# A spectral mixing layer and a SwiGLU block on one core: the back-transform's bursts in 512 columns, its clean-up at other places, and one load a step earlier

## The chip, the core and the metric

The kernel runs on one core of a Trainium2 chip. The metric is the device time of one execution in microseconds. Before the change it is 2777.25 us, the median of three runs (2773.95 to 2780.49). Engines are named as in the profile: PE is TensorE (PEld its weight loads, PEq its sequencer), DVE VectorE, ACT ScalarE, POOL GpSimd, SP SyncE, whose queue (SPq) issues most DMAs. All arithmetic is in float32, and each product that the program states is two matmul instructions in the trace.

## The reference

Two layers, one after the other. x has 8 batches of 3008 tokens with 256 channels.

```python
X = np.fft.rfft(x, axis=1)
y = np.fft.irfft(X * (filt_r + 1j * filt_i), n=3008, axis=1)   # along the tokens
t = y.reshape(24064, 256)
g = t @ w_gate                                                  # 256 -> 1536
out = (g * sigmoid(g) * (t @ w_val)) @ w_out                    # 1536 -> 256
```

## The kernel before

**Work.** A batch goes through two stages that overlap: while the feed-forward part of batch b runs, the spectral part of batch b + 1 is computed in small pieces between its products. The Fourier transform along 3008 = 47 x 64 tokens is split: the first stages (`quads`, `fours`, lines 715 to 881) go there, multiply by the filter and come back as far as a DRAM buffer of 48 x 64 rows (`d2`), and `back` (lines 1029 to 1066) does the last step for a quarter of a batch (a chunk). A batch has four chunks, and a chunk has three groups of hidden columns, so a batch is 12 steps, numbered 0 to 11. Each step is the same list of products: `P`, `Q` and the combinations `A`, `B`, `E` (L1134) make gate and value columns, and the `W` products (L1232) project hidden columns to the output. The products are a fast scheme in which sums of blocks replace some of the products, so DVE, ACT and POOL form sums between them.

**Order.** The order of every step is written by hand: `SCHEDULE` (lines 88 to 96) is a list of tokens, and the loop at line 1511 issues for each token its piece of work. Each engine executes what it gets in that order, and waits for other engines where data or space ask for it. A token with a prime belongs to the step before: its work is left over from there. Tokens that matter here: `h`, `v` are DVE products of hidden values (L1181); `x` and `s` make inputs of `A` on DVE (L1156); `l` (L312) and `e` (L316 or an ACT copy) do so for the `E` products; `S` are sums of hidden tiles on POOL (L309, L312); `n` are sums for the next chunk; `b0` to `b7` advance the spectral piece that this step carries (`quads` in steps 0 to 3, `fours` in steps 4 to 10, the first sums of a batch's x, `first_fold`, in step 11). Batches 0 to 5 have that last piece, and batch 7 has no next batch and carries none of these. In batch 0 the spectral work is arranged differently.

**`back`.** It is a generator of six pieces, called by the tokens `r0`, `r1` in the steps 0, 3 and 6 (for the chunks 1 to 3 of the same batch) and 10 (chunk 0 of the next batch), and by `r2'` to `r5'` in the step after. `r0`: a burst of small products (L1039): 24 rows by 32 columns of a constant table, in four row groups and four column groups of the array, into four PSUM banks. `r1`: DVE transposes two of the banks into the tile `y` (L1046), ACT copies the other two to `odd` (L1051). `r2'`: DVE transposes the two `odd` tiles (L1054). `r3'`, `r4'`: POOL adds and subtracts `odd` and `y` (L1059, L1061; in the profile under the helpers' lines L309 and L312). `r5'`: four more POOL sums on `y`. The tile `y` is first read by `n2` of the step 3k + 2 that precedes its chunk (step 11 for chunk 0). In batch 0 one call, for chunk 0 of batch 1, runs inside the `b` tokens of step 11. There are 28 calls: 21 in the batches 1 to 7, six in step 10 of the batches 1 to 6, and that one.

**Loads.** `load_t4` (lines 661 to 677) brings a chunk's rows of `d2` in two halves of four row blocks each, into two tiles of a pool with two buffers, one half per tile (`t4`). For chunks 1 to 3 the first half is issued at the start of the steps 0, 2 and 5, the second at `B01` of the same step; for chunk 0 of the next batch at `B01` and `A12` of step 10. Each half is four DMAs of 96 KB on SP's queue. `load_x(0)` (lines 615 to 625) loads a piece of x for a later batch: one DMA of 512 KB from a reordered copy (`turned`) and four of 128 KB from x, into a region of the tile `lent` that the filter of `fours` uses in steps up to 9. It is issued at `Q0`, the first token of step 11, and `first_fold` reads it on DVE at `b4` of the same step. SP's queue also carries the reloads of the weights (`wt_t`, L474, four pieces a step) and the stores of the results (L1217, twelve in a row in steps 1, 4, 7 and 10, after their DVE transposes at `z1.o'` and later).

Of the kernel before, what the change touches and what calls it, by code (L numbers as in the profile page):

```python
# [41 lines left out]
FP32 = mybir.dt.float32  # L42
# [6 lines left out]
B, S, C = 8, 3008, 256  # L49
# [5 lines left out]
NS, NQ = 24, 64  # L55
# [3 lines left out]
NH = 4  # L59
NW = 2 * NH  # L60
NCHUNK = 32 // NW
# [3 lines left out]
NG = 3  # L65
# [20 lines left out]


SCHEDULE = """
Q0 o3' z1.o' t4.2' W2 b0 f0 S00' S01' i0 b1 b2 x0.o' r2' t0.0 x1.o' i1 Q1 P0 t0.1 x2.o' P3 x3.o' f1 t4.3'
W1 x4.o' S10' x03 S11' D01 i2 i3 i4 s13 b3 x5.o' P1 o1 b4 t0.2 o2 z0.o c1 i5 A13 g1 c0 S20' Q2  # L90
S21' g0 y01 m13 t1.0 h0 f2 s01 W6 t1.1 h1 x23 D02 P2 o6 D12 A01 t0.3 i6 c2 i7 B13 i8 g2 i9 n3' m01
i10 S30' t1.2 i11 x02 W7 S31' g13 y12 r3' y02 B01 r4' h13 o7 t1.3 t2.0 s02 s12 g01 h2 b5 Q3 t2.1 h01 e12
A02 y23 W4 e02 b6 y03 m02 g3 A12 o4 z2.o t2.2 E12 m12 B02 t2.3 l12 e13 b7 E02 r5' u12 g02 t3.0 h3 s23
l02 B12 v12 E13 t3.1 h02 u02 A23 n2 l13 g12 v02 W5 s03 e23 h12 e01 m23 A03 o5 z3.o u13 E23 t3.2 m03
v13 E01 l23 e03 t3.3 t4.0 l01 u23 B23 v23 u01 E03 n1 t4.1 v01 g23 B03 l03 r0 W3 h23 g03 u03 r1 h03 v03
""".split()
KS = (-1, 0, 1, 2)

# [99 lines left out]
def kernel(  # L198
# [10 lines left out]
    nc = tc.nc  # L209
# [10 lines left out]
    def pool(name, bufs, space=None):  # L220
        kw = {} if space is None else {"space": space}
        return ctx.enter_context(tc.tile_pool(name=name, bufs=bufs, **kw))

    cpool = pool("consts", 1)
    xpool = pool("xp", 2)
    t1pool = pool("t1", 2)
    t4pool = pool("t4", 2)
    ypool = pool("yp", 2)
    wdpool = pool("wdram", 1, DRAM)
    wps = pool("wps", NB, PSUM)  # L230
# [3 lines left out]

    wt_t = cpool.tile([128, NPR, 2, 128], FP32)
    y_t = cpool.tile([128, 3 * len(PAIRS), TQ], FP32)

    lent = cpool.tile([128, 14 * NV * C], FP32)
    wt_1 = lent[:, 0:NPR * 256].rearrange("p (s z f) -> p s z f", z=2, f=128)
# [50 lines left out]
    pin = tc.keep_in_program_order  # L290
# [263 lines left out]
    back_t, quad_t = [], []  # L554
# [23 lines left out]
    class Spectral:  # L578
# [82 lines left out]
        def load_t4(self, k, i, part=None):  # L661
            at = 2 * k + i
            if part:
                self.load_rows(self.t4[k, i][8 * N_STORED:NK], k, slice(2 * N_STORED, NS), ts(i, NH))
                return
            t = t4pool.tile([128, NH, C], FP32, name=f"t4_{self.b}_{k}_{i}", tag="t4")
            if part == 0:
                self.load_rows(t[0:8 * N_STORED], k, slice(0, 2 * N_STORED), ts(i, NH), nc.gpsimd)
            elif self.b == 0:
                self.load_rows(t[0:NK], k, slice(0, NS), ts(i, NH))  # L670
            else:

                rows = self.d2_tokens.rearrange("(h n) (r s) c -> h r s n c", h=2, r=2)
                for part in range(4):
                    self.load(out=t[32 * part:32 * part + NS],
                              in_=rows[part // 2, part % 2, :, ts(at, NH)])
            self.t4[k, i] = t
# [351 lines left out]
        def back(self, k):  # L1029

            self.y[k] = y = ypool.tile([128, 8, TQ], FP32, name=f"y_{self.b}_{k}", tag="y")
            banks = [bank(f"pd_{self.b}_{k}_{part}") for part in range(4)]
            views = [t.rearrange("p (z i n d) -> p i z n d", z=2, i=2, d=32) for t in banks]
            for i in range(2):
                t = self.t4[k, i].rearrange("p n (z j d) -> p j z n d", z=2, d=32)
                for j in range(4):
                    for part in range(4):
                        r = slice(32 * part, 32 * part + NS)
                        pin(nc.tensor.matmul(  # L1039
                            out=views[part][32 * j:32 * j + 32, i], lhsT=back_t[0][r],  # L1040
                            rhs=t[r, j], start=i == 0, stop=True, skip_group_check=True))
            yield
            to = y.rearrange("p s n -> p (s n)").rearrange("p (z h m r) -> p h z m r", z=2, h=2, r=N1)
            odd = []
            for h in range(2):
                pin(nc.vector.transpose(  # L1046
                    out=to[:, h, :, :, 0:32],
                    in_=banks[2 * h].rearrange("p (z m r) -> p z m r", z=2, r=32)))
                t = xpool.tile([128, NV, C], FP32, name=f"odd_{self.b}_{k}_{h}", tag="x")
                odd.append(t.rearrange("p i c -> p (i c)"))  # L1050
                pin(nc.scalar.copy(out=odd[h], in_=banks[2 * h + 1]))  # L1051
            yield
            for t in odd:
                pin(nc.vector.transpose(out=t, in_=t))  # L1054
            yield
            for h in range(2):
                t = odd[h].rearrange("p (z m r) -> p z m r", z=2, r=32)
                n, low = slice(1 - h, 1 - h + N1 - NS), to[:, h, :, :, 0:NS]
                pin(sub(nc.gpsimd, to[:, h, :, :, N1 - 1:NS - 1:-1],  # L1059
                        to[:, h, :, :, n], t[:, :, :, n]))  # L1060
                pin(add(nc.gpsimd, low, low, t[:, :, :, 0:NS]))  # L1061
                yield
            for a in range(4):
                b, v = y[:, a], y[:, 4 + a]
                for _ in range(abs(KS[a])):
                    pin((sub if KS[a] > 0 else add)(nc.gpsimd, v, v, b))
# [191 lines left out]
    x0 = [t[0:NR, 8 * C * i:8 * C * i + 8 * C] for t, i in ((wo_f, 0), (wo_f, 1), (y_f, 0))]  # L1258
# [7 lines left out]
    with tc.tile_pool(name="start", bufs=1) as spool0:  # L1266
# [12 lines left out]
        n = 0  # L1279
# [174 lines left out]
    for b in range(B):  # L1454
# [38 lines left out]
        for step in range(NCHUNK * NG + (b == B - 1)):  # L1493
# [15 lines left out]
            last = ghost or b == B - 1 and step == NCHUNK * NG - 1  # L1509
            place = -1  # L1510
            for token in SCHEDULE:
                place += token[0] != "r"
                if b == 0 and this and place in tick_at[min(step, 3)]:
                    preparation.tick(step)
                old = token.endswith("'")
                op = token.rstrip("'")
                if (b, step) == (0, 0):
                    if op == "A01":
                        idle(wt_t[:, 0:2].rearrange("p s z f -> p (s z f)"),
                             [bank("idle") for _ in range(2)], 512)  # L1520
                    if op == "n2":
                        continue
                    if op == "n1":
                        preparation.finish(1)
                    elif op == "e23":
                        this.step("n2")
                if op[0] == "i":
                    if older is not None and older.b == 0:
                        older.project(op)
                elif op[0] == "t":  # L1530
                    n = int(op[1])
                    ps = pieces_before if old else pieces
                    if n < len(ps):
                        next(ps[n], None)
                elif op[0] == "r":
                    next(back_before if old else backs.get(step, gap), None)
                elif op[0] == "b":
                    next(bursts[step] if this else gap, None)
                elif op[0] in "Wo" or op.endswith(".o"):

                    g0 = older if old else before
                    if g0 is not None and (old or not ghost):
                        g0.project(op)
                else:
                    g0 = before if old else this
                    if g0 is not None and not (ghost and op[0] == "S"):
                        g0.step(op)
                if old or this is None:
                    continue
                if b == 0 and (step, op) == (5, "A23"):  # L1550
                    nxt.load_two(0)
                if b and b + 2 < B and (step, op) == (8, "Q0"):
                    following.turn_rows(0, 1, 2, 3)
                if b + 2 < B and (step, op) == (11, "Q0"):
                    following.load_x(0)
                if b == 1 and step < 4 and op in FILTER_AT:
                    n = FILTER_AT.index(op)
                    keep_filter(4 * step + n)
                if b and chunk and op == "B01":
                    cur.load_t4(chunk, 1)  # L1560
                for i in range(2):
                    if nxt and (step, op) == (10, ("B01", "A12")[i] if b else "E23"):
                        nxt.load_t4(0, i)
                for f, args in chores.get((step, op), ()) if b == 0 else ():
                    f(*args)
                if op in ends and not last and (b or step >= NT * NG - 1):
                    reload_weights((g + 1) % NG, ends[op])
# [35 lines left out]
```

## Time and profile before

| | |
|---|---|
| median of 3 runs | 2777.25 us |
| the profiled execution | 2773.0 us, of which span 2771.2 us |
| PE busy | 2728.7 us, 98% of the span |
| DVE, ACT, POOL busy | 75%, 55%, 63% |
| clock granted to PE over the span | 0.998 |
| `back` products, L1039 | 1792 matmul instructions of 24 x 256 (28 calls of 64), 42.7 us of PE |
| `quads` products, L725 | 768 of 24 x 512 (24 calls of 32), 27.4 us of PE |
| bytes moved by DMA | 608.47 MB, mean 220 GB/s |

Busy time of an engine is the union of its instructions. A row of the timeline is a run of equal instructions: its start, the time from the first start to the last end, line, tiles written and read, their number, and in brackets the idle time before it with what ended it. Matmuls are pipelined, so the distance from one row's start to the next says more than the second column. Idle time of an engine costs only where PE then waits for it.

### The profile page before, as it was taken

What the parts mean: (1) busy time and instruction counts of PE and PEld (TensorE: products, weight loads), DVE (VectorE), ACT (ScalarE), POOL (GpSimd) and SP (SyncE); (2) the same over time, 40 slices, a digit from 0 to 9 for tenths busy, and PEclk for the clock granted to TensorE, in tenths of its full rate; (3) what the DMA queues carried; (4) which work ended last, traced back from release to release, by engine and by line L of the source; (5) the groups of instructions that cost most, each with busy time, mean ns of one, the idle gap of its engine ahead of it and who ended that gap; (6) DMA issues with size and microseconds to landing.
All of it is one profiled execution on the core that took longest, in us unless ns stands there. A gap on an engine that the chain in (4) does not pass through costs nothing.

```text
span 2771.2 us, 51629 instructions
## 1 busy us (share of the span) xinstructions
PE 2728.7 (98%) x16952; PEld 2243.7 (81%) x16952; DVE 2082.3 (75%) x4703; ACT 1535.2 (55%) x4142; POOL 1758.0 (63%) x1909
## 2 busy tenths in 40 slices
PE   8999999999999999999999999999999999999998
PEld 6778887888877888788887888878887888888886
DVE  7788778777687777777778777777777777676666
ACT  5676455555555555555555555555555555555553
POOL 4777576676565766566765676566656566566553
PEclk9999999999999999999999999999999999999999
DMA  8688877877676776777767777668776777654443
GB/s 218 221 265 288 275 244 233 274 243 260 209 205 207 259 247 193 213 229 234 252 193 230 223 243 232 211 192 263 245 222 194 216 244 237 182 159 146 153 145 81
DMA packets 385312, 608.47 MB, mean 220 GB/s; under 512 B 199002, under 2 KB 268536, under 8 KB 384870
## 3 DMA queue, kind: packets, MB, share of 16 engines
q1 hardware_dynamic: 365833, 574.23, 66.0%
q10 hardware_dynamic: 16701, 25.56, 3.7%
q0 software_dynamic: 2512, 5.38, 0.7%
q8 instruction: 137, 2.24, 0.3%
q14 instruction: 129, 1.06, 0.1%
HBM read 484.44 MB, written 118.12 MB: 217 GB/s over the span
## 4 chain that ended last, share of the span: by engine, by line
PE 87%; DVE 4%; ACT 2%; DMA 2%; POOL 1%; issue 1%; SPq 0%; ACTq 0%; POOLq 0%; DVEq 0%
PE wa L1134 24%; PE wk L1134 16%; PE wA L1232 16%; PE we L1134 12%; PE wG L1232 8%; PE wF L1232 4%; PE wpd L1039 1%; PE wqc L805 1%; PE wqb L817 1%; PE wqa L725 1%; DVE we L312 1%; DVE y L316 0%; DVE lent L312 0%; DMA y<-y 0%; DVE h L1181 0%
## 5 line engine op out<-in xcount | busy, mean ns | idle before, releaser
L1134 PE MATMUL wa<-y_t,wt_t 128*128 128x188 f32 x4464 | 882.9, 324 | 15.8 <-DVE wa L1156 8.4
L1134 PEld LDWEIGHTS wa<-y_t,wt_t 128*128 128x128 f32 x4464 | 745.1, 190 | 105.2 <-PE wk L1134 16.6
L1134 PEld LDWEIGHTS wk<-y,wt_t 128*128 128x128 f32 x2976 | 497.3, 190 | 111.2 <-issue 27.5
L1134 PE MATMUL wk<-y,wt_t 128*128 128x188 f32 x2976 | 572.8, 325 | 0.0
L312 POOL TENSOR_TENSOR h<-h 128x376 f32<-128x376 f32 x572 | 561.4, 1003 | 15.1 <-DVE h L309 14.9
L1232 PE MATMUL wA<-h,wo_t 128*128 128x376 f32 x1532 | 548.3, 480 | 0.8 <-DVE o L309 0.7
L309 POOL TENSOR_TENSOR h<-h 128x376 f32<-128x376 f32 x190 | 183.5, 987 | 546.0 <-DVE h L1181 533.6
L1134 PE MATMUL we<-y_t,wt_t 128*128 128x188 f32 x2232 | 432.4, 323 | 2.4 <-DVE we L316 1.6
L312 POOL TENSOR_TENSOR D<-f,f 128x376 f32<-128x376 f32 x288 | 281.8, 990 | 225.2 <-ACT f L1149 219.3
L312 DVE TENSOR_TENSOR we<-we,m 128x376 f32<-128x376 f32 x576 | 317.9, 554 | 111.0 <-PE we L1134 98.1
L1134 PEld LDWEIGHTS we<-y_t,wt_t 128*128 128x128 f32 x2232 | 368.9, 190 | 5.0 <-DVE we L316 2.8
L1232 PEld LDWEIGHTS wA<-h,wo_t 128*128 128x128 f32 x1532 | 277.9, 190 | 102.9 <-POOL h L312 1.8
L1169 ACT COPY m<-wa 128x376 f32<-128x376 f32 x576 | 275.3, 478 | 91.9 <-PE wa L1134 87.4
L1176 ACT ACTIVATE u<-we 128x188 f32<-128x188 f32 x576 | 189.1, 328 | 178.0 <-DVE we L312 171.7
L1232 PE MATMUL wG<-h,wo_t 128*128 128x376 f32 x768 | 276.7, 483 | 0.0
L1176 ACT ACTIVATE g<-wa 128x188 f32<-128x188 f32 x576 | 187.4, 326 | 153.4 <-PE wa L1134 151.0
L316 DVE SCALAR_TENSOR_TENSOR y<-wk,c 128x376 f32<-128x376 f32 x480 | 247.4, 541 | 31.4 <-ACT c L1153 26.5
L1153 ACT COPY c<-wk 128x376 f32<-128x376 f32 x288 | 136.8, 475 | 235.3 <-PE wk L1134 226.7
L1149 ACT ACTIVATE f<-wk 128x376 f32<-128x376 f32 x288 | 144.4, 501 | 159.1 <-PE wk L1134 148.5
L1181 DVE TENSOR_TENSOR h<-we,u 128x188 f32<-128x188 f32 x576 | 199.0, 346 | 38.0 <-ACT u L1176 24.9
L1181 DVE TENSOR_TENSOR h<-wa,g 128x188 f32<-128x188 f32 x576 | 197.8, 344 | 33.8 <-ACT g L1176 33.5
L1165 ACT COPY we<-y 128x376 f32<-128x376 f32 x480 | 216.9, 481 | 5.3 <-DVE h L1181 4.0
(198 smaller groups left out, 3640.8 us busy)
## 6 DMA issues: line engine op xcount, KB each, us to landing
wt_t<-w_all SPq DMA_DIRECT2D x174, 896.0 KB
wt_t<-w_all SPq DMA_DIRECT2D x174, 768.0 KB
lent<-filter SPq DMA_DIRECT2D x36, 1024.0 KB
quads<-lent SPq DMA_DIRECT2D x96, 256.0 KB
d<-lent ACTq DMA_DIRECT2D x84, 256.0 KB
t<-d SPq DMA_DIRECT2D x224, 96.0 KB
lent<-quads SPq DMA_DIRECT2D x144, 128.0 KB
lent<-raw SPq DMA_DIRECT2D x144, 128.0 KB
```

What stands on the lines that cost most here:

```text
L309: return eng.tensor_tensor(out=dst, in0=a, in1=b, op=ALU.add)
L312: return eng.tensor_tensor(out=dst, in0=a, in1=b, op=ALU.subtract)
L316: return nc.vector.scalar_tensor_tensor(out=dst, in0=a, scalar=-1.0, in1=b, op0=ALU.mult, op1=ALU.subtract)
L725: pin(nc.tensor.matmul(out=banks[u, h][c:c + 32], lhsT=quad_t[0][r:r + NS, ts(t, 32)], rhs=parts[t][r:r + NS, ts(cp, NV * C)], start=True, ...
L1134: pin(nc.tensor.matmul(out=ps[:, z], lhsT=self.wt[:, SLOT[p], z], rhs=rhs, start=start and z == 0, stop=True, skip_group_check=True))
L1149: pin(act.mul(self.small(f"f{i}", f"f{i}", 1), t[f"k{i}"], -1.0))
L1153: pin(act.copy(out=self.small(f"c{i}", f"c{i}", 1), in_=t[f"k{i}"]))
L1165: pin(act.copy(out=self.bank(f"e{at}"), in_=t[f"y{at}"]))
L1169: pin(act.copy(out=self.small(f"m{at}", "m", 4), in_=t[f"a{at}"]))
L1176: pin(act.activation(out=self.small(op, "g", 3, 1)[:, 0], in_=ps[:, 1], func=AF.Silu))
L1181: pin(v.tensor_tensor(out=dst, in0=ps[:, 0], in1=g, op=ALU.mult))
L1232: pin(nc.tensor.matmul(out=self.tiles[at], lhsT=wo_t[:, JB * q + i, WO[p], :], rhs=self.hs[i][:, HID[p]], start=start and i == 0, stop=Tru ...
```

## The change

1. The two halves of a chunk's rows go into one constant tile `t4_t` with 2 x 4 row blocks, instead of two tiles from a pool. The places in memory are as large as before.
2. `r0` loops over the four column groups and four row groups only, and each product takes all eight row blocks: 512 columns instead of twice 256. That is 16 products (32 matmul instructions) per call where there were 32 (64). Each product needs both halves of the rows.
3. `r1` stands after `h03 v03`, the last two tokens of a step, instead of ahead of them.
4. `r2'` to `r5'` stand later in the steps 1, 4 and 7: `r2'` between `t2.3` and `l12`, `r3'` after `u12`, `r4'` after `v12`, `r5'` after `A23`. In step 11 they stay where they were, as tokens with a capital `R`, which do nothing in other steps.
5. `load_x(0)` is issued at `Q0` of step 10 instead of step 11 in the batches 1 to 5; in batch 0 it stays in step 11.

```diff
-Q0 o3' z1.o' t4.2' W2 b0 f0 S00' S01' i0 b1 b2 x0.o' r2' t0.0 x1.o' ...
+Q0 o3' z1.o' t4.2' W2 b0 f0 S00' S01' i0 b1 b2 x0.o' R2' t0.0 x1.o' ...
...
-i10 S30' t1.2 i11 x02 W7 S31' g13 y12 r3' y02 B01 r4' h13 o7 t1.3 ...
-A02 y23 W4 e02 b6 y03 m02 g3 A12 o4 z2.o t2.2 E12 m12 B02 t2.3 l12 e13 b7 E02 r5' u12 g02 t3.0 h3 s23
-l02 B12 v12 E13 t3.1 h02 u02 A23 n2 l13 g12 v02 W5 s03 ...
-v13 E01 l23 ... l03 r0 W3 h23 g03 u03 r1 h03 v03
+i10 S30' t1.2 i11 x02 W7 S31' g13 y12 R3' y02 B01 R4' h13 o7 t1.3 ...
+A02 y23 W4 e02 b6 y03 m02 g3 A12 o4 z2.o t2.2 E12 m12 B02 t2.3 r2' l12 e13 b7 E02 R5' u12 r3' g02 t3.0 h3 s23
+l02 B12 v12 r4' E13 t3.1 h02 u02 A23 r5' n2 l13 g12 v02 W5 s03 ...
+v13 E01 l23 ... l03 r0 W3 h23 g03 u03 h03 v03 r1
...
-    t4pool = pool("t4", 2)
...
+    t4_t = cpool.tile([128, 2 * NH, C], FP32)
...
-            t = t4pool.tile([128, NH, C], FP32, name=f"t4_{self.b}_{k}_{i}", tag="t4")
+            t = t4_t[:, ts(i, NH)]
...
-            views = [t.rearrange("p (z i n d) -> p i z n d", z=2, i=2, d=32) for t in banks]
-            for i in range(2):
-                t = self.t4[k, i].rearrange("p n (z j d) -> p j z n d", z=2, d=32)
-                for j in range(4):
-                    for part in range(4):
-                        r = slice(32 * part, 32 * part + NS)
-                        pin(nc.tensor.matmul(
-                            out=views[part][32 * j:32 * j + 32, i], lhsT=back_t[0][r],
-                            rhs=t[r, j], start=i == 0, stop=True, skip_group_check=True))
+            t = t4_t.rearrange("p n (z j d) -> p j z n d", z=2, d=32)
+            for j in range(4):
+                for part in range(4):
+                    r = slice(32 * part, 32 * part + NS)
+                    pin(nc.tensor.matmul(
+                        out=banks[part][32 * j:32 * j + 32].rearrange("p (z n d) -> p z n d", z=2, d=32),
+                        lhsT=back_t[0][r], rhs=t[r, j], start=True, stop=True))
...
-                elif op[0] == "r":
-                    next(back_before if old else backs.get(step, gap), None)
+                elif op[0] in "rR":
+                    if not old:
+                        next(backs.get(step, gap), None)
+                    elif (op[0] == "R") == (step == NCHUNK * NG - 1):
+                        next(back_before, None)
...
-                if b + 2 < B and (step, op) == (11, "Q0"):
+                if b + 2 < B and (step, op) == (10 + (b == 0), "Q0"):
                     following.load_x(0)
```

More of the change, by code (lines that the diff above doesn't have):

```diff
@@ L88 @@
 SCHEDULE = """
-Q0 o3' z1.o' t4.2' W2 b0 f0 S00' S01' i0 b1 b2 x0.o' r2' t0.0 x1.o' i1 Q1 P0 t0.1 x2.o' P3 x3.o' f1 t4.3'
+Q0 o3' z1.o' t4.2' W2 b0 f0 S00' S01' i0 b1 b2 x0.o' R2' t0.0 x1.o' i1 Q1 P0 t0.1 x2.o' P3 x3.o' f1 t4.3'
 W1 x4.o' S10' x03 S11' D01 i2 i3 i4 s13 b3 x5.o' P1 o1 b4 t0.2 o2 z0.o c1 i5 A13 g1 c0 S20' Q2
 S21' g0 y01 m13 t1.0 h0 f2 s01 W6 t1.1 h1 x23 D02 P2 o6 D12 A01 t0.3 i6 c2 i7 B13 i8 g2 i9 n3' m01
-i10 S30' t1.2 i11 x02 W7 S31' g13 y12 r3' y02 B01 r4' h13 o7 t1.3 t2.0 s02 s12 g01 h2 b5 Q3 t2.1 h01 e12
-A02 y23 W4 e02 b6 y03 m02 g3 A12 o4 z2.o t2.2 E12 m12 B02 t2.3 l12 e13 b7 E02 r5' u12 g02 t3.0 h3 s23
-l02 B12 v12 E13 t3.1 h02 u02 A23 n2 l13 g12 v02 W5 s03 e23 h12 e01 m23 A03 o5 z3.o u13 E23 t3.2 m03
-v13 E01 l23 e03 t3.3 t4.0 l01 u23 B23 v23 u01 E03 n1 t4.1 v01 g23 B03 l03 r0 W3 h23 g03 u03 r1 h03 v03
+i10 S30' t1.2 i11 x02 W7 S31' g13 y12 R3' y02 B01 R4' h13 o7 t1.3 t2.0 s02 s12 g01 h2 b5 Q3 t2.1 h01 e12
+A02 y23 W4 e02 b6 y03 m02 g3 A12 o4 z2.o t2.2 E12 m12 B02 t2.3 r2' l12 e13 b7 E02 R5' u12 r3' g02 t3.0 h3 s23
+l02 B12 v12 r4' E13 t3.1 h02 u02 A23 r5' n2 l13 g12 v02 W5 s03 e23 h12 e01 m23 A03 o5 z3.o u13 E23 t3.2 m03
+v13 E01 l23 e03 t3.3 t4.0 l01 u23 B23 v23 u01 E03 n1 t4.1 v01 g23 B03 l03 r0 W3 h23 g03 u03 h03 v03 r1
 """.split()
@@ L1511 @@
             for token in SCHEDULE:
-                place += token[0] != "r"
+                place += token[0] not in "rR"
                 if b == 0 and this and place in tick_at[min(step, 3)]:
```

## The prediction

> **What bounds the kernel.** I read the page first, then TensorE's waits, the chain, and the timelines of PE, DVE and SP around every place that the diff touches. All times are from the profiled execution (2773.0 us, span 2771.2), 4.25 below the median of the runs.
>
> ```profile
> span 2771.2 us, 51629 instructions
> PE 2728.7 (98%) x16952; PEld 2243.7 (81%) x16952; DVE 2082.3 (75%) x4703; ACT 1535.2 (55%) x4142; POOL 1758.0 (63%) x1909
> ```
> PE is the bound: a saving counts if it shortens PE's own work or one of its few waits. The largest wait of PE is
>
> ```profile
> PE wa L1134 <- DVE wa L1156: 8.4, 14, 1.5
> ```
> 14 waits for `s` tokens. The chain shows the price of a `back`: in batch 7, without other spectral work, the same 12 products recur once a step.
>
> ```profile
> 2444.07 1.91 PE wk L1134 x12
> ...
> 2471.08 1.91 PE wk L1134 x12
> ...
> 2496.48 1.91 PE wk L1134 x12
> ```
> A step with `back` takes 27.01 us, the next, which holds `r2'` to `r5'`, 25.40: `back` costs PE 1.61, its later pieces nothing there. The two kinds of burst, before (`back`) and a relative (`quads`), on PE's timeline:
>
> ```profile
> 1747.37 1.49 PE L1039 MATMUL wpd<-t,back 24*32 24x256 f32 x64
> 1748.79 1.53 PE L1232 MATMUL wG<-h,wo_t 128*128 128x376 f32 x4
> ```
>
> ```profile
> 1776.33 1.43 PE L1232 MATMUL wF<-h,wo_t 128*128 128x376 f32 x4
> 1777.68 1.14 PE L725 MATMUL wqa<-lent,quad 24*32 24x512 f32 x32
> 1778.75 2.18 PE L1134 MATMUL wk<-y,wt_t 128*128 128x188 f32 x12
> 1780.77 0.48 PE L1232 MATMUL wA<-h,wo_t 128*128 128x376 f32 x1
> ```
> The reader is to see that the 24x512 burst, exactly the shape of the new one, holds PE for 1.07 from its start to the next row, the old one for 1.42.
>
> **Change 1 and 2: the burst.** Slot of `quads`: 1776.33 to 1780.77 is 4.44; four W matmuls take 1.27 and twelve wk 1.91 elsewhere; 1.26 is left. Slot of `back`: 1.61. Difference 0.35, times 28 calls: **9.8 us**. Why it is so, by single starts in the trace: 16 tiles of the array run together, starting 7 ns apart; a pass of 16 takes 0.216 (second pass, 1747.61 to 1747.82) at 256 columns and 0.453 at 512 (`quads`, first pass). So streaming is the same; gone is the hole between the halves, 1747.82 to 1748.01, where the second half's four loads are waited for, and one filling. The moving operand is strided (runs of 32 floats) where that of `quads` is contiguous; but the old burst's second pass ran 256 strided columns in 0.216, the rate of `quads`, so I cost the stride at nothing.
>
> The Trainium skill's page TensorEngine Tiling (Array Packing), section Key Properties, speaks against the change: a switch of tiling mode drains the array. The trace agrees: the next full-size matmul starts 0.30 after the last start of the old burst, 0.52 after that of `quads`, so longer products make the drain longer by 0.21. Without a drain, the saving would be 0.56 a call and 15.8 in all; the rows above hold it already.
>
> The Trainium skill's TensorE: Matmul & The Clock Gate, section "Wait — 56ns, not 53.3ns?", says starts are never closer than about 25 ns; 32 fewer instructions would be worth 0.8 a call, 22 us in all. The rows' 7 ns contradict it, and I keep 0.35.
>
> What the trace can't show: all eight waits for loads now come ahead of the first products. Before, four stood there as waits of PE's sequencer (0.05 each, issued 0.125 apart, the last one 0.94 before the burst) and four hung on weight loads in the middle. Four more at 0.125 use 0.5 of the 0.94: nothing lost. Bounds of the call's gain: 0.56, were the drain no longer than before; and 0.35 - 4 x 0.125 = -0.15, were the waits not hidden. I take 0.35, whose row has the same shape. Range of the part: -4 to +16.
>
> Loads themselves: the tightest is step 10, where SP issues the eight `t` from 1732.57 to 1737.57 and the burst starts at 1747.37; a similar load of 256 KB on POOL's queue lands in 4.7. That the first products now need both halves costs nothing with 5 us in hand. Each half has the same place in memory as before, so what a new load waits for, the burst several steps back, is long past.
>
> **Change 3: `r1` after `h03 v03`.** The two `h`, `v` (0.34 each) wait for nothing while DVE idles ahead of the burst's end, so they go ahead of the transposes; ACT's order is unchanged. The banks come free no later, as the burst ends 0.35 sooner. 0; were that cover gone, 0.7 later transposes, against `quads` 3.3 after the burst: still 0.
>
> **Change 4: `r2'` to `r5'`.** DVE in step 1 of batch 5, old place:
>
> ```profile
> 1810.09 1.30 DVE L1054 STREAM_TRANSPOSE odd<-odd 128x512 f32<-128x512 f32 x2
> 1811.31 0.51 DVE L1156 SCALAR_TENSOR_TENSOR x<-wk,f 128x376 f32<-128x376 f32 x1
> 1811.75 0.55 DVE L1156 SCALAR_TENSOR_TENSOR wa<-wk,f 128x376 f32<-128x376 f32 x1
> ```
> and PE behind it:
>
> ```profile
> 1812.44 0.88 PE L1134 MATMUL wa<-y_t,wt_t 128*128 128x188 f32 x4 [0.42 <-DVE wa L1156]
> ```
> The transposes hold DVE for 1.22 just ahead of `s13`, for which PE waits. Counted over the usual distance of two matmuls (0.159), PE loses 0.59 there and 0.07 at the next matmul, in step 1 of the batches 1 to 6: 6 x 0.66 = **4.0**. In step 7 the same place loses 0.31: **1.9**. Steps 4 and batch 7 lose nothing. At the new place DVE has, in step 1 of batch 5:
>
> ```profile
> 1823.31 0.56 DVE L312 TENSOR_TENSOR we<-we,m 128x376 f32<-128x376 f32 x1 [1.27 <-PE we L1134]
> 1823.78 0.55 DVE L316 SCALAR_TENSOR_TENSOR we<-wk,c 128x376 f32<-128x376 f32 x1
> ```
> It idles 1.27 until PE has made `E12`, and 1.96 at this place in steps 4, 7 and all of batch 7. The 1.22 fit in. Behind them `l12` and `e13` queue; `E13` on PE (1824.95) reads `e13`, done at 1824.33: 0.62 to spare. POOL's sums, about 6 us, move from 13 us into a step to 19; POOL idled 6.2 before the next step's `S` sums in step 1 (2.3 to 2.6 in 4 and 7, where the spectral sums that followed move forward instead). It ends near 26.5, the `S` start near 27; `y` isn't read before `n2` of the following step. No queue of DMAs is passed. 0; bounds: the old stalls simply move (-5.9), or every one of 21 places loses 1.22 - 0.62 = 0.60 (-12.6).
>
> **Change 5: `load_x(0)`.** In step 11 of batch 1, DVE at `b4`:
>
> ```profile
> 758.61 0.69 DVE L309 TENSOR_TENSOR lent<-lent 128x512 f32<-128x512 f32 x1 [1.77 <-DMA lent<-in_x_dram]
> ```
> PE then loses a microsecond at `s13` and half a one later: the step takes 27.44, against 25.53 in batches 2 to 4, where the load is in time. Batch 5 waits 1.32 and takes 27.01. Gain 1.91 + 1.48 = **3.4**; 0 in batch 0. On SP's queue its five DMAs pass a whole step of weights, `t` and result stores. Their new place:
>
> ```profile
> 1720.85 0.32 SPq L474 DMA_DIRECT2D wt_t<-w_all  x1
> 1723.77 8.25 SPq L1217 DMA_DIRECT2D out_dram<-o  x12
> ```
> SP stands waiting for 2.6 before the stores, and the five need 2.5. The 1 MB lands within 8 to 10, ahead of the stores and beside the `d` stores; if all behind is 5 us later, `t` still has its landing. 0 taken; bounds: 0, and 5 batches x 5 us.
>
> **Sum:** 9.8 + 4.0 + 1.9 + 3.4 = 19.1. 2773.0 - 19.1 = 2753.9 for the profiled execution; against the median 2777.25 - 19.1 = **2758**.
>
> **Rivals.**
> - *The stall moves.* DVE reaches the transposes late and `E13` waits: 0.60 x 21 = 12.6 back, 6.5 gained, 2771; half of it, 2765. For: `l12` and `e13` stand directly behind; step 0 already loses 0.4 at `E13`. Against: 1.96 idle in 15 places of 21.
> - *The burst gains nothing,* the waits in front take its 0.35: 9.3 gained, 2768. For: eight waits at one place; against: the sequencer runs 0.9 ahead.
> - *Slower: PE's sequencer runs out of lead.* In the burst at 1747.37 the fourth wait came 0.91 after the third. If four more come at 0.7 to 0.9, less the lead of 0.94, a call loses 1.9 to 2.7; 28 x 1.9 = 53, less 19.1: +34, 2811. It decides from 0.68 a call on (19.1 / 28); 0.88 makes 0.2% slower. Against: three waits passed at 0.125, and the fourth most likely met a full queue, which waits don't fill.
> - *Chunk 0's rows late* in step 10: five batches; it eats the gain at 3.8 us past its landing each.
>
> **How the numbers follow.** As worked out: 0.60. Stall moves: 0.16 (2765 to 2771). Burst gains nothing: 0.09 (2764 to 2771). Slower: 0.08, of which late rows 0.03. Mixtures that leave it within 0.2% (5.5 us, about what a measurement can tell): 0.07. Faster 0.84 (the first three, less a hundredth), same 0.08, slower 0.08. Likeliest case's own range, with drain and second-order waits: 2753 to 2763; with the others 2750 to 2771.
>
> **What would show it.** L1039 at 896 matmuls of 24x512, next row 1.07 after its start; batch 7's step with `back` at 26.65; no PE wait at `s13` in steps 1 and 7 (27.0 and 27.5 long instead of 27.70 and 27.79); L1054 in the idle time ahead of `l12`; no DMA wait of `first_fold` in batches 1 and 5. Wrong: more sequencer waits with a gap of PE before L1039, a PE wait for `we` L316, or a later `t`.

## The result, and the profile after

The changed kernel takes 2752.74 us (median of five runs, 2747.74 to 2759.66) against 2777.25 (2771.31 to 2781.19 in the same five rounds): ratio 0.9914, 95% interval 0.9891 to 0.9937. Measured again beside two variants it was 2753.28, ratio 0.9915 (0.9901 to 0.9928). The forecast was 2758, with 2750 to 2771 as its range. The profiled executions are 2773.0 us before and 2754.7 after, their spans 2771.2 and 2752.9.

The page after, its head and TensorE's costliest group:

```profile
span 2752.9 us, 49865 instructions
PE 2716.0 (99%) x16056; PEld 2228.0 (81%) x16056; DVE 2089.3 (76%) x4703; ACT 1533.2 (56%) x4142; POOL 1752.5 (64%) x1909
...
L1132 PE MATMUL wa<-y_t,wt_t 128*128 128x188 f32 x4464 | 881.5, 323 | 9.3 <-ACT m L1167 4.4
```

PE has 896 matmul instructions less (28 x 32), is busy 12.7 us less, and its idle time ahead of the `wa` products fell from 15.8 to 9.3. The wait for DVE at the `s` tokens, once the largest of PE, is now

```profile
PE wa L1132 <- DVE wa L1154: 2.3, 4, 0.7
```

The chain in batch 7, the same recurring products as in the prediction:

```profile
2427.30 1.91 PE wk L1132 x12
...
2453.96 1.91 PE wk L1132 x12
...
2479.36 1.91 PE wk L1132 x12
```

26.66 with `back`, 25.40 without: a call costs 1.26 instead of 1.61, exactly the slot of `quads`. The burst itself on PE's timeline, in step 10 of batch 4:

```profile
1737.56 1.14 PE L1037 MATMUL wpd<-t_t,back 24*32 24x512 f32 x32
1738.63 1.53 PE L1230 MATMUL wG<-h,wo_t 128*128 128x376 f32 x4
```

1.07 from its start to the next row, as forecast. DVE at the new place of the second transposes, in step 1 of batch 5:

```profile
1809.87 0.54 DVE L316 SCALAR_TENSOR_TENSOR y<-wk,c 128x376 f32<-128x376 f32 x1
1810.33 1.29 DVE L1052 STREAM_TRANSPOSE odd<-odd 128x512 f32<-128x512 f32 x2
1811.77 0.56 DVE L312 TENSOR_TENSOR we<-we,m 128x376 f32<-128x376 f32 x1 [0.15 <-PE we L1132]
1812.24 0.55 DVE L316 SCALAR_TENSOR_TENSOR we<-wk,c 128x376 f32<-128x376 f32 x1
```

Of 1.27 us of idle time 0.15 are left; `l12` still waits for PE, not PE for it. And `first_fold` in step 11 of batch 1 finds its data:

```profile
755.83 0.55 DVE L309 TENSOR_TENSOR o<-o,wA 128x376 f32<-128x376 f32 x1 [0.18 <-PE wA L1230]
756.29 1.02 DVE L309 TENSOR_TENSOR lent<-lent 128x512 f32<-128x512 f32 x1
```

Where the time went, by steps (length of a step: from PE's first product in it to its first product in the next, counted off PE's instructions; the lengths agree between batches to 0.05 where one number is given):

| step | before | after | in the batches | sum |
|---|---|---|---|---|
| 0, 3, 6, 10 (with `back`) | 29.19, 28.38, 29.10, 28.24 | 28.84, 28.02, 28.75, 27.89 | 27 calls in 1 to 7 | -9.5 |
| 10, an extra hold-up | 0 | 0.47, 0.50 | 4, 5 | +1.0 |
| 1 | 27.70 (batch 1: 27.95) | 26.66 (26.81) | 1 to 6 | -6.3 |
| 7 | 27.79 | 27.48 | 1 to 6 | -1.9 |
| 11 | 27.44, 27.01 | 25.53 | 1, 5 | -3.4 |
| 2 | 27.50, 25.70 | 27.36, 25.43 | 5, 7 | -0.4 |
| start and batch 0 | 443.8 | 446.2 | | +2.4 |

With rounding and the end that is the -18.3 of the two spans. All other steps are unchanged to 0.05 us. Step 2 in batches 5 and 7 is shorter by the same amounts in e3 below (change 5 alone) and not in e1, e2 and e4, so it came with the load's new place; but e8 has the old lengths and e11 the new ones, and the wait behind it stays open.

The two hold-ups of step 10 have different causes. In batch 4 ScalarE's copies come late (rows further down). In batch 5 the rows of chunk 0 come late. The load of x now stands ahead of the stores of the results on SP's queue, these took longer than the 8.26 us that they took there before, and the eight `t` are issued behind them:

```profile
2045.37 11.17 SPq L1215 DMA_DIRECT2D out_dram<-o  x12
2057.09 5.33 SPq L597 DMA_DIRECT2D t_t<-d  x8
```

```profile
2067.22 1.64 PE L1037 MATMUL wpd<-t_t,back 24*32 24x512 f32 x32
2068.79 0.90 PE L1230 MATMUL wG<-h,wo_t 128*128 128x376 f32 x2
```

The last `t` is issued 4.80 us before the burst, where the kernel before had 8.1 to 9.8 in these batches. Three of the burst's waits in PE's sequencer take 0.49, 1.24 and 0.55 us instead of 0.05, the burst stands still for 0.44 behind its third matmul, and it holds PE for 1.57 instead of 1.07.

### The profile page after: what moved, and what is told of

Read it like the earlier page. It is cut to its first block, busy times and chain, and to the rows that moved or that the text cites. A ratio compares the mean times of both kernels' runs of the same rounds, so it can differ in the third digit from the quotient of the medians.

```text
span 2752.9 us, 49865 instructions
## 1 busy us (share of the span) xinstructions
PE 2716.0 (99%) x16056; PEld 2228.0 (81%) x16056; DVE 2089.3 (76%) x4703; ACT 1533.2 (56%) x4142; POOL 1752.5 (64%) x1909
## 4 chain that ended last, share of the span: by engine, by line
PE 86%; DVE 3%; POOL 2%; ACT 2%; DMA 2%; issue 1%; SPq 0%; ACTq 0%; POOLq 0%; DVEq 0%
PE wa L1132 24%; PE wk L1132 17%; PE wA L1230 16%; PE we L1132 12%; PE wG L1230 8%; PE wF L1230 4%; PE wqc L805 1%; PE wqb L817 1%; PE wpd L1037 1%; PE wqa L725 1%; POOL h L312 1%; POOL out_dram L1215 0%; DVE y L316 0%; DVE we L312 0%; DVE h L1179 0%
```

## The experiments

Lengths of steps are read from one profiled execution each. In the batches they repeat so well that 0.1 us shows, while whole executions of one kernel differ by 10 us.

### Each part alone

Four kernels: the one before, with one part of the diff.

```diff
# e1: changes 1 and 2
-    t4pool = pool("t4", 2)
+    t4_t = cpool.tile([128, 2 * NH, C], FP32)
...
# e2: change 4
-... x0.o' r2' t0.0 ... y12 r3' y02 B01 r4' h13 ... E02 r5' u12 g02 ...
+... x0.o' R2' t0.0 ... y12 R3' y02 B01 R4' h13 ... t2.3 r2' l12 ... E02 R5' u12 r3' g02 ...
...
# e3: change 5
-                if b + 2 < B and (step, op) == (11, "Q0"):
+                if b + 2 < B and (step, op) == (10 + (b == 0), "Q0"):
# e4: change 3
-... h23 g03 u03 r1 h03 v03
+... h23 g03 u03 h03 v03 r1
```

> The kernel before with changes 1 and 2 alone: 512-column bursts from one constant tile. My theory: each call in the batches 1 to 7 gives back 0.35 us of TensorE, and nothing else moves, so steps 0, 3, 6 and 10 are 0.35 shorter (batch 7: 27.02 to 26.66) and step 1 stays at 27.70, step 7 at 27.79, step 11 of batch 1 at 27.44. Sum 27 x 0.35 = 9.5, less up to 0.6 for the call in batch 0, whose rows arrive late: 9 to 10. Rival: part of the shorter steps seen after the change came from change 3 (the first transposes behind h03 and v03); then these steps lose clearly less than 0.35 here.

> The kernel before with change 4 alone: later places of the second transposes and the sums. My theory: step 1 of the batches 1 to 6 falls from 27.70 to 26.66 (1.04, not the 0.66 that I forecast), step 7 from 27.79 to 27.48 (0.31), the rest stays: 6 x 1.35 = 8.1. Rival: the fall of 1.04 needs the shorter burst or the earlier h03, v03 too; then step 1 stays at about 27.04 here.

> The kernel before with change 5 alone: the first load of x in step 10. My theory: step 11 falls to 25.53 in batch 1 (by 1.91) and batch 5 (by 1.48); step 10 of some batches is up to 0.5 longer than 28.24, where the second store on ScalarE's queue takes 1.4 us to issue instead of 0.6 and ScalarE's copies come late. Together -2.4 to -3.4. Rival: the longer step 10 has another cause (the constant tile, the shorter burst) and is not seen here.

> The kernel before with change 3 alone: the first transposes behind h03 and v03. My theory: nothing, each step of the batches 1 to 7 within 0.05 us of before. Rival: later free banks hold up the next burst at the start of the steps 1, 4 and 7, or earlier h and v free TensorE: 0.1 us or more in these steps.

| step (batch) | before | e1 burst | e2 moves | e3 load | e4 `r1` | after |
|---|---|---|---|---|---|---|
| 0 (7) | 27.02 | 26.66 | 27.02 | 27.02 | 27.02 | 26.66 |
| 3 (4) | 28.38 | 28.02 | 28.37 | 28.38 | 28.38 | 28.02 |
| 1 (4) | 27.70 | 27.70 | 26.67 | 27.70 | 27.70 | 26.66 |
| 7 (4) | 27.79 | 27.79 | 27.48 | 27.79 | 27.79 | 27.48 |
| 10 (4) | 28.24 | 27.89 | 28.24 | 28.54 | 28.24 | 28.36 |
| 11 (1) | 27.44 | 27.16 | 26.84 | 25.53 | 27.05 | 25.53 |
| 11 (3) | 25.53 | 26.91 | 26.75 | 25.53 | 26.41 | 25.53 |
| 11 (5) | 27.01 | 26.94 | 26.95 | 25.53 | 26.58 | 25.53 |

In the regular steps the parts are independent. The burst gives 0.35 to 0.36 a call and touches nothing else; the moves alone take 1.04 from step 1, so neither the shorter burst nor change 3 is needed for that; change 3 alone moves nothing. Step 1 of batch 1 is not regular: 27.95 before, 28.09 in e1, 28.41 in e4, 27.39 in e2 and 26.81 after, so there the moves alone gave half of the fall. The load alone makes step 11 regular, and it brings batch 4's hold-up of step 10 with it: 28.54 with nothing else changed.

The last three rows hold a surprise. With the load in step 11, its lateness is not tied to batches 1 and 5: the wait hits two to four of the five batches in the executions before, e1, e2, e4 (and e5, e6 below), and costs 2.9 to 5.8 us in all (3.4 in the one execution that I predicted from); with the load in step 10 it never came, in six executions (after, its repetition, e3, e8, e9, e10). So this part is worth some 4 us on the average, less what step 10 loses by it (0 to 1.0).

### Why a burst of half as many products is shorter

I had explained 0.19 of the 0.35 us by waits: the second half's rows are waited for on weight loads in the middle of the old burst. e6 moves these waits to the front, by four tiny products that read the second half, with the burst as before.

```diff
+            for part in range(4):
+                r = slice(32 * part, 32 * part + NS)
+                pin(nc.tensor.matmul(out=banks[part][0:32, 0:4], lhsT=back_t[0][r],
+                                     rhs=self.t4[k, 1][r, 0, 0:4], start=True, stop=True))
             for i in range(2):
...
-                            rhs=t[r, j], start=i == 0, stop=True, skip_group_check=True))
+                            rhs=t[r, j], start=True, stop=True, skip_group_check=True))
```

> The kernel before with four tiny products of 4 columns, one for each row group, ahead of the burst: they read the second half of the rows, so all waits for rows stand in front of the burst as they do after the change, while the burst keeps 64 instructions of 256 columns. (They are overwritten, and the result is the same.) Theory: 0.19 us of the 0.35 is the hole between the halves, where the second half's rows are waited for on the weight loads. Then the step of batch 7 with back is shorter by 0.19 less the tiny products' own time (8 instructions in one pass, 0.05 to 0.15): 26.88 to 27.0; the step after the change has 26.66. Rival: the hole isn't the waits, but the change of half itself: then the tiny products come on top, 27.07 to 27.2.

Against the expectation, e6 computes other values; number, shape and order of the products are as it says, and only their times are used. Batch 7's steps with `back` take 27.08, 0.06 more than before. In the trace the pause is still there, 0.19 us (0.526 to 0.713 us after the burst's first start), now behind the 41st matmul instruction, with the eight tiny ones counted, and behind it the products start 17 ns apart as before. So the waits for rows were not its cause. Two more kernels ask what is: the new burst twice in a row, and the old burst in two halves with the W3 products between them.

```diff
# e10, on the kernel after
-            for j in range(4):
+            for j in (0, 1, 2, 3, 0, 1, 2, 3):
# e11, on the kernel before
             for i in range(2):
+                if i:
+                    yield
...
-... l03 r0 W3 h23 g03 u03 r1 h03 v03
+... l03 r0 W3 r0 h23 g03 u03 r1 h03 v03
```

> The changed kernel with its 512-column burst done twice in a row (same result): 64 matmul instructions as before the change, but of 512 columns. What is open: why the old burst stood still for 0.19 us after its 33rd instruction and then started one matmul every 17 ns instead of every 7, also where all waits for rows stood in front. Theory (supply): TensorE had about 64 instructions (32 weight loads and 32 matmuls) ready when the burst began, used them up at 7 ns each, and then ran at the pace of its sequencer; products of 512 columns take 27 ns each on the average (0.43 us for a pass of 16), which the sequencer can follow. Then the second 32 cost two passes more, 0.86 to 0.90 us, and the step of batch 7 with back goes from 26.66 to 27.52 to 27.56. Rival: a hold-up of 0.19 us comes with every burst beyond 32 matmuls, of whatever length: 27.71 or more.

> The kernel before with the burst's two halves apart: the first half where it was, the second behind the W3 products (1.26 us of TensorE), each 32 matmul instructions of 256 columns. Theory (supply): each half finds its instructions ready; no hole, all starts 7 ns apart within a pass, each half 0.64 us from its first start to the next row (0.24 + 0.10 + 0.30), and with 0.19 us for entering and leaving, 2 x 0.83 = 1.67: the step of batch 7 with back is 27.07, against 27.02 before and 26.66 after. So fewer instructions in one burst, not their number in all, is what pays, and splitting gives it away again by a second drain. Rival: the second half stands still because its weight loads wait for rows: then its starts show the hole here too, and the step is 27.2 or more.

The timeline of PE in batch 7, first e10, then e11:

```profile
2475.97 2.35 PE L1037 MATMUL wpd<-t_t,back 24*32 24x512 f32 x64
2478.25 1.53 PE L1230 MATMUL wG<-h,wo_t 128*128 128x376 f32 x4
```

```profile
2491.40 0.71 PE L1041 MATMUL wpd<-t,back 24*32 24x256 f32 x32
2492.04 1.53 PE L1234 MATMUL wG<-h,wo_t 128*128 128x376 f32 x4
2493.50 0.71 PE L1041 MATMUL wpd<-t,back 24*32 24x256 f32 x32
2494.15 0.90 PE L1136 MATMUL wk<-y,wt_t 128*128 128x188 f32 x4
```

e10 is 2.28 from its start to the next row, 1.21 more than the single burst, where my supply theory allowed 0.90; the step is 27.87, as the rival had it (27.71 or more). Start times in the trace (ns from the burst's first):

| | matmuls 1 to 32 | the 33rd | the 34th | from there |
|---|---|---|---|---|
| before, 256 columns | 7 apart, passes at 0 and 240 | 455 | 649 | 17 apart |
| e10, 512 columns | 7 apart, passes at 0 and 453 | 882 | 1076 | 17 apart, the last 15 from 1527 on |
| e11, each half | 7 apart, passes at 0 and 240 | | | |
| after | 7 apart, passes at 0 and 453 | | | |

Both theories fall in part. The pause of 0.194 comes behind the 33rd matmul instruction at 256 and at 512 columns (the rival was right there; the refill during the long passes, which I had assumed, does not happen); but the slow starts behind it, 17 ns, cost too, and the rival had left them out. That they are the pace at which instructions arrive fits, but no run shows it by itself. At full pace two more passes of e10 would cost 0.88 of the 1.21; 0.33 is left for the pause and the slow starts. e11 settles the waits: its second half waits for the same rows on the same weight loads, and shows neither pause nor slow starts. Its step is 26.98 (27.07 expected): the second drain costs about what the pause and the slow starts cost. Steps 1 and 4 behind it are 0.91 longer, since the four banks are filled later; 25 us are lost in all, so it is no way to go.

One more rival is that the pause comes where the 16 tiles of the array are used for a third time in a row. The `fours` in the kernel before speak against it: a burst of 32 matmul instructions there (L805 and L817, 64 x 64, at 1584.52) goes over four tiles in eight rounds, with starts at 0, 267 and 483 ns and so on every 216, without such a pause.

So what the new burst saves is: the pause, 0.194; the slow starts of the second half, 1120 - 649 = 471 ns instead of the 340 ns that a half takes at full pace, 0.131; and 0.028 of the rest. So what costs is the part of a burst beyond 32 instructions; what lies behind that number is argued. What PE has ready when a burst begins may be 32 matmul instructions and their 32 weight loads. The Trainium skill's page TensorE: Matmul & The Clock Gate gives 64 as the depth of TensorE's queue in the table at its head; that agrees with the count before and in e10, not with e6, where the pause came eight instructions later. No run shows the queue itself, and why the refill begins so late stays open.

### Whether the sums of `y` matter in step 1

```diff
-... x0.o' R2' t0.0 ... t2.3 r2' l12 ...
+... x0.o' r2' t0.0 ... t2.3 l12 ...
```

> The kernel before with only the sums r3' to r5' moved; the second transposes r2' stay at their old place. Theory A: the whole 1.04 us of step 1 and 0.31 us of step 7 come from the transposes standing in VectorE's order ahead of the inputs of A: step 1 stays at 27.70 and step 7 at 27.79. Theory B: TensorE's second wait in step 1 (at 11.1 us into it, 0.37 us) comes from GpSimd's sums of y beside VectorE's sums: then step 1 falls to about 27.33 here and step 7 stays. VectorE's sums of x (1.2 us where they meet the sums of y, 0.7 us else) should become 0.7 us long at that place by either theory.

All steps are as before: 27.70 and 27.79. The second statement was wrong: POOL's sums did not move at all. In the trace they begin 13.90 us into step 1 in both kernels, because a token's place orders an instruction only within its own engine's list, and POOL has nothing else there. They move, to 16.74, when the transposes move that they wait for. So e5 does not test theory B by itself; the order of time does, since PE's second wait stands at 11.1, ahead of all these sums. The transposes are left as the cause of both waits.

### How much room the transposes have at the new place

```diff
             for t in odd:
-                pin(nc.vector.transpose(out=t, in_=t))
+                for _ in range(3):
+                    pin(nc.vector.transpose(out=t, in_=t))
```

> The changed kernel with each of the second transposes done three times (same result), so that they hold VectorE for 3.7 instead of 1.2 us at every call. Theory: at the new place there are, after the change, 0.15 us of idle VectorE behind them and 0.62 us before E13 needs e13 in step 1, and 0.76 + 0.62 in step 4, 7 and all of batch 7. The extra 2.5 us then cost TensorE 1.7 in step 1 (26.66 to 28.4), 1.1 in step 4 (26.62 to 27.7), in step 7 (27.48 to 28.6) and in steps 1, 4 and 7 of batch 7 (25.40 to 26.5). Step 11, where they stand at the old place, pays too, by an amount that I don't forecast. Rival: they are hidden with much more room, and these steps grow by less than half of that.

The timeline of DVE and then of PE in step 1 of batch 4:

```profile
1506.70 0.54 DVE L316 SCALAR_TENSOR_TENSOR y<-wk,c 128x376 f32<-128x376 f32 x1
1507.16 4.28 DVE L1053 STREAM_TRANSPOSE odd<-odd 128x512 f32<-128x512 f32 x6
1511.36 0.53 DVE L312 TENSOR_TENSOR we<-we,m 128x376 f32<-128x376 f32 x1
1511.79 0.55 DVE L316 SCALAR_TENSOR_TENSOR we<-wk,c 128x376 f32<-128x376 f32 x1
```

```profile
1509.61 0.80 PE L1133 MATMUL wa<-y_t,wt_t 128*128 128x188 f32 x4
1512.40 1.34 PE L1133 MATMUL we<-y_t,wt_t 128*128 128x188 f32 x4 [1.99 <-DVE we L316]
1513.53 1.46 PE L1133 MATMUL wa<-y_t,wt_t 128*128 128x188 f32 x4
1514.78 2.10 PE L1231 MATMUL wG<-h,wo_t 128*128 128x376 f32 x4
```

PE waits at `E13` for `e13`, as the rival had it. Six transposes that depend on each other in pairs take 4.20 from start to next, 2.95 more than two, not 2.5. In batch 7, steps 1, 4 and 7 take 27.05: 1.65 longer, against 2.95 - 0.76 - 0.62 = 1.57. The margins are close to those read: 0.15 + 0.62 in step 1, 0.76 + 0.62 elsewhere. Step 1 of batch 4 grew by 3.94, though, to 30.60, where 2.95 - 0.15 - 0.62 = 2.2 explain the wait. The rest is clock, in the windows around the wait:

```profile
1500.00:1512.00 12.00, 10.41 (x55) 1.00 0.78 251
1512.40:1515.80 3.40, 3.40 (x10) 0.55 0.47 124
1515.80:1521.00 5.20, 5.20 (x29) 0.97 1.06 244
```

(The columns are the window, its length, PE's busy time and matmuls, the granted clock, the DMA share and GB/s.) After this stop PE got about half its clock for 3.4 us, and four products took 1.25 instead of 0.64. The same followed the stops of 1.99 to 2.27 us in step 1 of the batches 2, 3, 5 and 6. It did not follow the stop of 2.27 us in step 1 of batch 1, which took 29.20, 2.39 more than after the change, about what the wait explains, nor any stop of 1.4 us in the other steps.

### The load behind the chunk's rows, and a place for `n2`

```diff
# e8, on the kernel after
-                if b + 2 < B and (step, op) == (10 + (b == 0), "Q0"):
+                if b + 2 < B and (step, op) == ((10, "A12") if b else (11, "Q0")):
# e9, on e8
-... A23 r5' n2 l13 g12 v02 W5 s03 e23 ...
+... A23 r5' l13 g12 v02 W5 s03 n2 e23 ...
```

> The changed kernel once more, beside the two that follow. Theory: the steps of the batches 1 to 7 come out as before to 0.05 us, except step 10, where the hold-up of ScalarE (0.5 us) meets other batches or none; the start (70 to 75 us until the first product of step 0) and batch 0 (367 to 371 us) move by a few us from one execution to the next, and make the spread of the times. Rival: the long start and batch 0 (75.3 and 370.9 us) belong to the change; then they come back here.

> The changed kernel with the first load of x issued at A12 of step 10, behind the rows of chunk 0, instead of at Q0. Theory: the load no longer meets the two stores on ScalarE's queue, so step 10 is 27.89 in all batches, and it still has 15 us before it is read, so step 11 stays at 25.53: 0 to 1 us faster than the changed kernel. Rival: it now comes too late or holds up the weights behind it: step 11 above 25.6 or the next step 0 above 28.9 in some batch.

> The same, with n2 (two ScalarE copies and the GpSimd sums for the next chunk) behind s03 instead of ahead of it. Theory: the wait of TensorE for ScalarE's copy to the bank of an A product in step 2 (0.32 us at 22.2) and step 11 (0.13 us) goes: step 2 at 27.04, step 11 at 25.40, about 6 x 0.45 = 2.7 us in all, and 2751 or less in the median. Rival: the sums for the next chunk come late and the next step's A13 or A02 waits: steps 0, 3, 6 or 9 get longer.

The changed kernel again: all steps of the batches 1 to 7 to 0.05 us, with the hold-up of step 10 only in batch 4 (28.32). Start and batch 0 came back as 75.06 and 369.50; among all executions here they range from 70.5 to 76.4 and from 367.1 to 374.3. So the start isn't the change's. In batch 0 one thing is: its only burst, in step 11, begins before its last rows have landed, and now needs them all. In PE's sequencer two waits for rows take 1.29 us (at 413.82) and 0.67 us (at 415.18) in the kernel after; the kernel before had 0.05 each. That burst holds PE 2.96 us until the next row instead of 2.35 (2.19 to 2.64 in the kernel before, e2, e3, e4 and e5; 2.96 to 3.17 in the one after, its repetition, e1, e8 and e9). The rest of batch 0's 2.1 us was not settled.

e8: step 10 is 27.89 in all batches and step 11 stays 25.53, as expected; 2753.59 (ratio to the kernel before 0.9916, 0.9902 to 0.9929), no difference from the changed kernel that such runs can show. e9: step 11 25.40 as expected, step 2 27.16 instead of 27.04 (27.40 in batch 3), steps 5 and 8 0.03 shorter; 2749.73, ratio 0.9908 (0.9895 to 0.9922). By steps, e9, which has e8's load too, beats the changed kernel's repetition by about 2.5 us; the interval of the ratio does not separate them.

## Why the prediction was right

The time, 2752.74, lies in the range, 5 us under the likeliest value and at the lower end of the likeliest case's own 2753 to 2763. Step by step:

- **The burst, 9.8:** right, 27 x 0.35 = 9.5 in the batches, and 0.6 lost in batch 0's call. The row of equal shape, `quads`, gave the size to 0.01. The reason given beside it was wrong: "the hole between the halves, where the second half's four loads are waited for". e6 and e11 show the hole without the waits and the waits without the hole; it comes in bursts of more than 32 matmul instructions.
- **The drain and the 25 ns:** the drain is as read (0.52 after the last start). Starts 7 ns apart were seen in every burst, and 17 behind the 33rd, both below the 25 that the prediction quotes from the Trainium skill's page TensorE: Matmul & The Clock Gate, section "Wait — 56ns, not 53.3ns?".
- **Waits in front:** "nothing lost" held wherever the rows had landed. The sequencer has four waits a burst, some of them for two semaphores, not eight. The rival of a sequencer without lead did not come.
- **Both halves needed:** "costs nothing" held for 26 calls. The call in batch 0 lost 0.6; the prediction had only step 10 in view. And step 10 of batch 5 lost 0.50: the "5 us in hand" were worked out from the old places of the loads, and change 5 used them up. That is the rival *Chunk 0's rows late*, in one of five batches and at a small price, with the later `t` that was named as a sign of being wrong.
- **Change 3, 0:** right in the regular steps (e4).
- **Change 4, 4.0 + 1.9:** mis-sized in the first term, which measured 6.3. I counted PE's wait at the place of the transposes, 0.66, and took the next wait, 0.37 at 11.1 us, for one that steps 0 and 2 have anyway. It came with the same transposes: e2 takes it away, and step 1 has no wait left. That it is DVE's backlog behind them is argued. Step 7's 1.9 is exact. The place ahead of `l12` has the room that I read, with 0.15 us to spare in step 1; e7 shows what it costs to overrun it. POOL's sums went from 13.90 us into step 1 to 16.74, not to 19, since they follow their transposes.
- **Change 5, 3.4:** exact for the profiled execution, by chance: the wait falls on other batches in other executions. "0 taken" for the new place missed 1.0 us in the profiled execution: the late rows in batch 5, and 0.47 in batch 4. There ScalarE's queue issues two stores beside the load; the second took longer, and ACT's copies came late. ACT after, batch 4:

```profile
1716.84 2.04 ACTq L857 DMA_DIRECT2D d<-lent  x2
1718.97 0.51 ACT L1246 COPY o<-wA 128x376 f32<-128x376 f32 x1 [2.55 <-DMA lent<-in_x_dram]
```

 The two issues take 2.04 where they took 1.50 in the kernel before; PE then loses 0.47 at `f`. It came in batch 4 of three of the five executions with the load at `Q0` of step 10, and in none with the load elsewhere. I had asked what is queued on SP behind the load, and not what else issues DMAs in these microseconds; and for what is queued behind it, "`t` still has its landing" was 0.50 us short in one batch. In e8, with the load behind `t`, neither came.
- **The sum, 19.1:** the profiled spans give 18.3, the medians 24.5. That 18.3 is so near is in part luck: 2.3 more from change 4 and 0.4 from step 2 stand against 1.0 lost in step 10 and 2.4 in the start and batch 0. Part of the gap may be the execution that I started from: two late loads, while others had up to four. The start's 5 us of play hides the rest; it isn't settled.

## What to carry to other kernels

On an engine that is busy all the time, price a burst by a burst of the same shape that is already in the trace, from the row before it to the row after it; its busy time and the count of its instructions say less. By these runs, many small products that run side by side in the array are best kept to 32 matmul instructions in a row with float32 weight loads between them, made as long as they go. Work moved out of a busy engine's list belongs directly ahead of an instruction that waits for the bottleneck anyway, and a long load belongs well before its use even when most executions get by without, but behind the loads on the same queue that are needed sooner (e8).

## What was not expected of the hardware

- **A burst has 32 matmul instructions at full pace.** Behind the 33rd: 0.194 us of pause, then 17 ns from start to start instead of 7, for products of 256 and 512 columns alike (before, e10); two bursts of 32 show neither (e11). With eight tiny products ahead it was the 41st (e6).
- **A stop of PE of 2 us can cost its clock too.** After five of six stops of 1.99 to 2.27 us PE got about half its clock for 3.4 us (e7; 0.55 in the window shown); after one of 2.27 us, and after those of 1.4 us, it kept it.
- **DVE's sums of two tiles slow down beside POOL's.** `lent<-lent` of 128 x 512 takes 0.67 to 0.73 us where POOL forms no sum beside it (44 of 96 before), and 0.68 to 1.29 where it does; in step 1 before, beside POOL's sums of `y`, it took 1.20, and after the change, with these sums later, 0.68. In batch 0's step 11 after, one took 2.18. The Trainium skill's page SBUF — State Buffer, section Who interferes with whom, says that a DVE instruction with two SBUF inputs and a GpSimd instruction that reads SBUF contend; the times agree. It cost PE nothing in step 1.
- **A DMA issue can hold up the engine that issues it.** The second of two stores on ACT's queue took 1.40 us to issue instead of 0.60, 4 to 6 us after SP had issued 1 MB of loads (after, batch 4), and ACT's next copy came behind it.
